# A new order for the first third of an RWKV block with a squared-ReLU feed-forward, and a last product in two column runs

## The chip, the cores and the metric

The kernel runs on one core of one Trainium2 chip. The metric is the device time of one execution, in microseconds (us); lower is better. TensorE (PE) multiplies matrices, VectorE (DVE) and ScalarE (ACT) read its results out of PSUM, GpSimd (POOL) works on SBUF alone and issues some DMAs, SyncE (SP) issues most of them.

## What is computed

```python
# attention part: B, H, S, D = 4, 8, 768, 48
for t in range(S):
    kt, vt, rt = k[:, :, t], v[:, :, t], r[:, :, t]
    cur = np.einsum('bhd,bhe->bhde', u[None] * kt, vt)
    y[:, :, t] = np.einsum('bhd,bhde->bhe', rt, state + cur)
    state = w[None, :, :, None] * state + np.einsum('bhd,bhe->bhde', kt, vt)

# feed-forward part on x = y as [3072 tokens, 384]: w_in [384, 2048], w_out [2048, 384]
h = np.maximum(x @ w_in, 0.0)
out = h * h @ w_out
```

Inputs and the output are float32; the matrix products run in bf16 with float32 sums.

## The kernel before

**Units.** The sequence is cut into 6 chunks of 128 steps; with 4 batches that makes 24 units of 128 tokens and all 8 heads. Unit i is batch i % 4, chunk i // 4, so units 0 to 3 start from a zero state and unit i needs the state that unit i - 4 left. The recurrence is done per unit as small matrix products. The steps of one unit i are:

- `ld.r.i`, `ld.k.i`, `ld.v.i`: loads of 192 KB each (pieces of 192 bytes), on SyncE's queue
- `rh.i`, `kh.i`: r and k times the decay tables, into bf16; `P0.i`, `P1.i`, `du.i`, `dv.i`: the term of the step's own token (r*k, times u, summed, times v); `vb.i`: v in bf16
- `T.i` (eight transposes on TensorE) and `Tc.i` (their copy out of PSUM), or `XB.i` (a transposing DMA) in their place for later units; `A.i` (eight products), `Bm.i.0`, `Bm.i.1` (their mask), `Y.i` (the unit's output), `U.i` (its share of the state), `S0`/`ts`/`S` (the state's update)
- `xs.i` adds the own-token term; `X.i` and `xTc.i`, or the DMA `xX.i`, bring the result into the layout that the feed-forward part needs

**Feed-forward part.** Units are grouped (`GROUPS`: two groups of one unit, then eleven of two). `F1.g.s` computes 512 columns of `x @ w_in` into one PSUM bank: 12 products of 128 columns for a group of one, 6 products of 256 columns for a group of two. `re.g.s` is the ReLU out of PSUM, `sq.g.s` the square. `F2.i.q` is a quarter of unit i's second product: four matmuls of 384 columns; four quarters sum into one bank, `os.i` copies it out and `out.i` stores it.

**Weights.** `w_in` is eight pieces W1[0..7]. `lW.0.s` loads a piece as float32 on SyncE's queue (384 KB, four buffers `wsa`) and `cW.0.s` casts it; piece 2 comes by `W.0.2`, a casting DMA that GpSimd issues. `w_out` is four pieces by `W.1.0` to `W.1.3`, all casting DMAs of GpSimd. F1 of a one-unit group's piece s needs W1[2s] and W1[2s+1], F1 of a two-unit group's piece s needs W1[s]; `F2.i.q` needs W.1.q.

**What sets the order.** `ORDER` is one written-out list of all steps. A token reads `what:engine/buffers`: `A.1:P/1/2` is step A of unit 1 on TensorE into PSUM buffers 1 and 2; the engine letters are A (ScalarE), D (VectorE), G (GpSimd), P (TensorE) and S (SyncE's DMA queue); a D or A with a digit picks a form of `sq`. Each engine runs its steps in the list's order and waits at a step until the data and the buffer that it names are ready. PSUM has four general buffers (`bank`), two for F1 (`bankH`) and two for F2 (`bankO`). `Z.n.b` are n dummy products into a bank, which only keep TensorE working in the first microseconds.

The last unit to finish is 22. Its four quarters run last on TensorE. Its eviction is cut in two halves of 192 columns, `os.22.0` on ScalarE and `os.22.1` on VectorE, both out of the same PSUM bank, with a store behind each.

## Time and profile before

| | |
|---|---|
| three runs | 175.53, 175.57, 176.38 us; median 175.57 |
| the profiled execution: span from first to last instruction | 174.6 us; the runs' median is 0.9 us longer than this span |
| granted TensorE clock, mean | 0.998 |
| busy: PE, DVE, ACT, POOL | 164.3, 140.6, 109.4, 69.4 us |
| DMA traffic | 28.36 MB, mean 162 GB/s |
| SyncE's queue | 72.6% of the 16 DMA engines' span |
| GpSimd's queue | 6.3% |
| first F1 product starts | 21.63 us into the span |
| last product ends | 171.09 us into the span |

The profile's times are microseconds from the first instruction. PE is the row of matrix products, PEld that of the weight loads into the array, which overlap them. The 40 slices are equal parts of the span, with busy shares in tenths. A line of a timeline has the start, the length, the engine and the line of the kernel, and in brackets the idle time before it and what ended it. A DMA's landing is when its last engine reports.

### The profile page before, as it was taken

What the parts mean: (1) busy time and instruction counts of PE and PEld (TensorE: products, weight loads), DVE (VectorE), ACT (ScalarE), POOL (GpSimd) and SP (SyncE); (2) the same over time, 40 slices, a digit from 0 to 9 for tenths busy, and PEclk for the clock granted to TensorE, in tenths of its full rate; (3) what the DMA queues carried; (4) which work ended last, traced back from release to release, by engine and by line L of the source; (5) the groups of instructions that cost most, each with busy time, mean ns of one, the idle gap of its engine ahead of it and who ended that gap; (6) DMA issues with size and microseconds to landing.
All of it is one profiled execution on the core that took longest, in us unless ns stands there. A gap on an engine that the chain in (4) does not pass through costs nothing.

```text
span 174.6 us, 4605 instructions
## 1 busy us (share of the span) xinstructions
PE 164.3 (94%) x1813; PEld 127.1 (73%) x1813; DVE 140.6 (80%) x279; ACT 109.4 (63%) x203; POOL 69.4 (40%) x85
## 2 busy tenths in 40 slices
PE   3978599999999999999999999999999999999991
PEld 3967488866778777877767787777778677787760
DVE  5779677799899989999989898899988667853620
ACT  3578479549499987786677669669478142164410
POOL 5253834044366594925373960700950302000000
PEclk9999999999999999999999999999999999999999
DMA  4989999989799999999998989989931422110041
GB/s 99 228 194 240 320 200 237 207 155 213 144 205 177 231 217 165 233 157 252 152 214 187 195 164 220 160 196 230 164 94 26 158 90 71 24 45 4 0 165 61
DMA packets 102421, 28.36 MB, mean 162 GB/s; under 512 B 94840, under 2 KB 102400, under 8 KB 102400
## 3 DMA queue, kind: packets, MB, share of 16 engines
q1 hardware_dynamic: 100504, 26.20, 72.6%
q0 software_dynamic: 1744, 1.77, 6.3%
q8 instruction: 14, 0.23, 0.5%
q10 hardware_dynamic: 152, 0.10, 0.2%
q14 instruction: 7, 0.06, 0.1%
HBM read 20.46 MB, written 4.72 MB: 144 GB/s over the span
## 4 chain that ended last, share of the span: by engine, by line
PE 84%; DMA 6%; SPq 4%; POOL 1%; issue 1%; ACT 0%; DVE 0%; POOLq 0%
PE bank L472 36%; PE bank L445 36%; DMA wsa<-in_moe_w_in_dram 6%; SPq L320 4%; PE bank L376 3%; PE bank L394 2%; PE bank L392 2%; PE bank L403 2%; PE bank L363 2%; PE bank L429 1%; POOL W L262 1%; SPq L324 0%; POOL urow L218 0%; ACT vb L260 0%; DVE os L262 0%
## 5 line engine op out<-in xcount | busy, mean ns | idle before, releaser
L445 PE MATMUL bank<-xT,W 128*128 128x256 bf16 (+1 forms) x624 | 74.4, 264 | 2.3 <-ACT W L260 2.1
L472 PE MATMUL bank<-W,hq 128*128 128x384 bf16 x384 | 73.6, 326 | 0.0
L453 ACT ACTIVATE hr<-bank 128x512 bf16<-128x512 f32 x71 | 42.0, 597 | 36.8 <-PE bank L445 34.2
L445 PEld LDWEIGHTS <-W 128*128 128x128 bf16 x624 | 55.4, 98 | 12.6 <-ACT W L260 2.2
L472 PEld LDWEIGHTS <-hq 128*128 128x128 bf16 x384 | 35.6, 98 | 17.8
L460 ACT ACTIVATE hq<-hr 128x512 bf16<-128x512 bf16 x57 | 34.7, 629 | 2.5 <-DVE hr L455 2.2
L384 DVE TENSOR_TENSOR Bm<-bank,maskJT 128x512 bf16<-128x512 f32 x48 | 31.4, 682 | 3.1 <-PE bank L376 3.0
L346 POOL TENSOR_TENSOR P<-P,ub 128x384 f32<-128x384 f32 x14 | 15.2, 1087 | 30.2 <-DVE P L342 27.4
L354 POOL TENSOR_TENSOR dv<-ldv,du 128x384 f32<-128x384 f32 x19 | 16.4, 874 | 25.0 <-DVE du L349 21.0
L455 DVE TENSOR_SCALAR hr<-bank 128x512 bf16<-128x512 f32 x25 | 17.1, 688 | 11.2 <-PE bank L445 7.5
L464 DVE TENSOR_TENSOR hq<-hr 128x512 bf16<-128x512 bf16 x35 | 15.0, 456 | 1.7 <-ACT hr L453 1.7
L411 DVE TENSOR_TENSOR xs<-bank,dv 128x384 bf16<-128x384 f32 x24 | 13.2, 553 | 3.2 <-PE bank L394 2.5
L481 PE MATMUL bank<-identity 128*128 128x128 bf16 x139 | 11.1, 244 | 2.7 <-POOL identity masks.py:199 2.7
L260 ACT COPY os<-bank 128x384 f32<-128x384 f32 (+1 forms) x18 | 8.4, 469 | 8.1 <-PE bank L472 8.1
L342 POOL TENSOR_TENSOR P<-ldr,ldk 128x384 f32<-128x384 f32 x11 | 11.3, 1025 | 4.8 <-DMA ldr<-in_r_dram 4.8
L349 DVE TENSOR_REDUCE du<-P 128x8 f32<-128x384 f32 x24 | 12.9, 542 | 0.0
L260 ACT COPY rkT<-bank 128x1024 bf16<-128x1024 bf16 x10 | 10.1, 1016 | 3.4 <-PE bank L363 3.3
L481 PEld LDWEIGHTS <-identity 128*128 128x128 bf16 x139 | 9.8, 112 | 2.9 <-POOL identity masks.py:199 2.7
L424 POOL TENSOR_TENSOR S0W<-ts,WLm 128x384 bf16<-128x384 f32 x7 | 7.4, 1061 | 10.0 <-PE bank L472 6.7
L394 PE MATMUL bank<-vb,Bm 128*128 128x48 bf16 x192 | 10.8, 183 | 0.5 <-ACT vb L260 0.5
L394 PEld LDWEIGHTS <-Bm 128*128 128x128 bf16 x192 | 9.5, 96 | 1.5 <-issue 0.8
L260 ACT COPY xT<-bank 128x384 bf16<-128x384 bf16 x14 | 6.5, 478 | 5.1 <-PE bank L429 5.1
(62 smaller groups left out, 167.1 us busy)
## 6 DMA issues: line engine op xcount, KB each, us to landing
ldr<-in_r_dram SPq DMA_DIRECT2D x24, 192.0 KB, 3.8
ldk<-in_k_dram SPq DMA_DIRECT2D x24, 192.0 KB, 3.9
ldv<-in_v_dram SPq DMA_DIRECT2D x24, 192.0 KB, 3.6
out_dram<-os SPq DMA_DIRECT2D x23, 192.0 KB, 2.1
wsa<-in_moe_w_in_dram SPq DMA_DIRECT2D x7, 384.0 KB, 5.9
W<-in_moe_w_out_dram POOLq DMA_DIRECT2D x4, 384.0 KB, 7.6
rkT<-rk SPq DMA_TRANSPOSE x14, 4.2
W<-in_moe_w_in_dram POOLq DMA_DIRECT2D x1, 192.0 KB, 8.8
```

The costliest lines, as they stand in the source:

```text
L260: e.copy(o, a)
L346: e.tensor_mul(t, t, ub)
L354: e.tensor_mul(dvb[slot[f"dv{i}"]], loaded("v", i), t)
L384: e.tensor_mul(Bmb[slot[f"Bm{i}{h}"]], heads(bank(f"bA{i}{h}"), 128), mask_b)
L394: e.matmul(y[:, hc, D * h : D * (h + 1)], m[h][:, hc, :], vb[:, 2 * hc + h, :], start=(c == 0), stop=True, skip_group_check=True,)
L445: e.matmul(hp[:, fi, :], W1[f // 2][:, c, 128 * (f % 2) : 128 * (f % 2 + 1)], xt[:, c, :], start=(c == 0), stop=(c == CCH - 1), skip_group ...
L453: e.activation(hr, hp, AF.Relu)
L455: e.tensor_scalar_max(hr, hp, 0.0)
L460: e.activation(hq, hr, AF.Square)
L464: e.tensor_mul(hq, hr, hr)
L472: e.matmul(bank(f"bO{i}", "bO")[:, 0:d_model], hqb[slot[f"hq{g},{f // m}"]][:, at : at + L], W2[q][:, f % 4, :], start=(f == 0), stop=(f = ...
L481: e.matmul(banks[b][:, 0:128], identity, identity, start=True, stop=True, skip_group_check=True)
```

## The change

1. The list `ORDER` is new from its beginning to about `F1.5.1` (a third of all steps). Behind that each engine has the same steps in the same order, with other buffer numbers. The count of dummy products is the same, 139; six of them now stand behind F1.1.0. Some 70 steps of the first third move to another engine: GpSimd has 89 steps where it had 72, ScalarE 189 where it had 204. All loads are on SyncE's queue, as they were, in a new order.
2. `F2.22.0` to `F2.22.3` are replaced by `F2c.22.0` and `F2c.22.1`: the whole sum of 16 matmuls for columns 0 to 255, then for columns 256 to 383, in two PSUM banks. Each is copied out and stored by itself, and `os.23` and `out.23` stand between.

The beginning of the list before, to the last product of units 0 and 1:

```
ld.r.1:S/0 w:A ld.k.1:S/0 u:S Z.48.5:P tab:A ld.k.0:S/1 ld.k.2:S/2 shw:D ld.r.0:S/1 logw:A ld.r.2:S/2 Wt:A/0 P0.1:D/0
shu:D Wk:A/1 lW.0.6:S/0 rh.1:D/0 kh.1:D ld.v.1:S/0 ld.k.3:S/3 T.1:P/0 kh.0:D/1 Z.16.5:P P1.1:G Tc.1:A/0 kh.2:D/2 rh.0:D
ld.v.3:S/1 WtS:A rh.2:D P0.2:G/1 A.1:P/1/2 WkS:A T.0:P/3 lW.0.1:S/1 Z.16.5:P P1.2:D ld.r.3:S/3 Tc.0:A/1 du.1:D/0
P0.0:D/2 cW.0.6:A ld.v.0:S/2 A.0:P/0/3 dv.1:G Bm.1.1:D/0 Z.6.5:P du.2:D/1 T.2:P/2 P1.0:G Bm.1.0:D/1 ld.v.2:S/3 Z.22.5:P
Tc.2:A/2 Bm.0.0:D/2 Bm.0.1:D/3 lW.0.0:S/2 vb.1:A/0 lW.0.5:S/3 kh.3:D/3 Y.1:P/1 cW.0.1:A lW.0.7:S/0 A.2:P/0/2 xs.1:D/0
Z.4.5:P P0.3:G/3 vb.3:A/1 du.0:D/2 lW.0.4:S/1 X.1:P/3 Z.8.5:P rh.3:D wc:S xTc.1:A/0 Bm.2.0:D/4 vb.0:A/2 T.3:P/1
ld.k.4:S/4 dv.0:D Y.0:P/3 Z.13.5:P Tc.3:A/3 vb.2:G/3 Bm.2.1:D/5 P1.3:G xs.0:D/1 A.3:P/0/2 X.0:P/1 cW.0.0:A U.0:P/3
dv.2:G Bm.3.0:D/1 Z.6.7:P xTc.0:A/1 du.3:D/3 lW.0.3:S/2 F1.1.0:P/0 Bm.3.1:D/0 ld.r.4:S/4 F1.0.0:P/1 re.1.0:D/0 W.1.0:G
W.0.2:G cW.0.7:G Y.2:P/0 Y.3:P/1 re.0.0:A/1 ld.k.5:S/5 xs.2:D/2 cW.0.5:A dv.3:D F1.1.3:P/0 cW.0.4:A X.2:P/2 F1.0.3:P/1
re.1.3:D/2 ld.r.5:S/5 xTc.2:A/0 W.1.1:G U.2:P/0 xs.3:D/3 F1.0.2:P/0 re.0.3:A/3 sq.1.3:D2/0 WLcol:A X.3:P/2 F1.1.2:P/1
re.0.2:D/4 xTc.3:A WLm:G U.3:P/1 F1.2.1:P/0 re.1.2:A/5 W.1.2:G sq.0.3:A0/1 F1.2.5:P/1 re.2.1:D/2 W.1.3:G sq.0.0:A0/2
U.1:P/2 S0.2:D re.2.5:A/3 F1.2.4:P/0 sq.0.2:D2/3 cW.0.3:A S0.0:D F1.2.7:P/1 re.2.4:D/1 sq.1.0:A0/4 F2.0.0:P/1
sq.2.5:D2/5 re.2.7:A/4 S0.3:D F1.0.1:P/0 F1.2.3:P/1 re.0.1:D/0 F2.1.0:P/0 S0.1:D re.2.3:A/3 F1.1.1:P/0 sq.1.2:D2/6
sq.0.1:D2/7 ld.k.7:S/6 F1.2.0:P/1 re.1.1:A/5 F2.0.1:P re.2.0:A/0 sq.1.1:D2/8 F1.2.2:P/0 sq.2.4:A0/9 sq.2.0:D1/10
F2.1.1:P kh.4:D/4 F1.2.6:P/1 ld.v.5:S/4 rh.4:D P0.4:D/4 F2.1.2:P ld.r.7:S/6 re.2.2:D/5 P1.4:G F2.0.2:P re.2.6:D/1
sq.2.2:A0/11 F2.1.3:P ld.v.4:S/5 kh.5:G/5 sq.2.1:A0/12 sq.2.6:D1/13 F2.0.3:P os.1:A/0 du.4:D/4 ld.k.6:S/0 T.4:P/0
...
```

and the same stretch after:

```
w:A tab:A ld.r.2:S/0 ld.k.3:S/0 shw:D ld.r.1:S/1 logw:A Wk:A/0 Z.48.4:P Z.22.5:P ld.r.0:S/2 Wt:A/1 u:S rh.1:D/0
ld.k.1:S/1 shu:D kh.1:D rh.2:D/1 WtS:A T.1:P/0 ld.k.2:S/2 ld.k.0:S/3 Z.13.4:P rh.0:D/2 Tc.1:A/0 P0.1:G/0 ld.r.3:S/3
kh.3:D/3 lW.0.1:S/0 A.1:P/1/2 Z.16.5:P Z.4.4:P P1.1:G kh.0:D T.0:P/3 P0.2:G/1 wc:S lW.0.0:S/1 ld.v.1:S/0 Bm.1.1:D/0
ld.v.0:S/1 P0.0:G/2 lW.0.6:S/2 P0.3:G/3 kh.2:D P1.3:G Tc.0:A/1 Z.16.5:P Bm.1.0:D/1 rh.3:D du.1:D/0 T.2:P/0 ld.v.2:S/2
vb.1:A/0 Tc.2:A/2 A.0:P/2/3 Z.8.4:P lW.0.5:S/3 Bm.0.1:D/2 T.3:P/1 dv.1:G cW.0.0:A WLcol:A Z.6.5:P P1.2:D P1.0:G
Bm.0.0:D/3 vb.0:G/1 Y.1:P/0 du.0:D/1 A.2:P/3/2 xs.1:D/0 du.2:D/2 dv.0:G WLm:G Bm.2.1:D/4 ld.v.3:S/3 X.1:P/0 Y.0:P/2
Bm.2.0:D/5 xs.0:D/1 du.3:D/3 cW.0.1:A U.0:P/3 xTc.1:A/0 Tc.3:A/3 vb.2:G/2 lW.0.7:S/1 A.3:P/2/0 X.0:P/1 S0.0:D F1.1.0:P/0
Bm.3.0:D/1 cW.0.6:G vb.3:A/3 dv.2:G xTc.0:A/1 cW.0.5:G Y.2:P/3 lW.0.4:S/0 WkS:A U.3:P/2 Bm.3.1:D/0 re.1.0:A/0 cW.0.7:A
U.1:P/1 F1.0.0:P/1 xs.2:D/2 ld.r.4:S/4 dv.3:G ld.k.4:S/4 Y.3:P/0 W.0.2:G cW.0.4:G kh.4:G/4 S0.3:D Z.6.4:P lW.0.3:S/2
re.0.0:A/1 X.2:P/3 W.1.0:G F1.1.3:P/0 xs.3:D/3 ld.k.5:S/5 F1.0.3:P/1 sq.1.0:D2/0 W.1.1:G rh.4:D sq.0.0:D2/1 W.1.2:G
X.3:P/2 xTc.2:A/0 cW.0.3:G re.1.3:A/2 F1.0.2:P/0 ld.r.5:S/5 ld.v.4:S/4 re.0.3:A/3 xTc.3:A sq.0.3:D2/2 re.0.2:A/4
F1.1.2:P/1 W.1.3:G ld.v.5:S/5 T.4:P/0 F1.2.1:P/0 kh.5:G/5 P0.5:G/4 re.1.2:D/5 sq.1.3:D2/3 P0.4:G/0 Tc.4:A/4 re.2.1:D/0
F1.2.5:P/1 A.4:P/3/2 sq.2.1:D2/4 re.2.5:A/1 F1.2.7:P/0 F1.2.4:P/1 re.2.7:A/3 U.2:P/0 re.2.4:A/2 F1.0.1:P/0 F1.1.1:P/1
ld.k.6:S/6 sq.1.2:D2/5 sq.0.2:D2/6 ld.r.6:S/6 Bm.4.1:D/3 rh.5:D Bm.4.0:D/2 P1.4:G re.0.1:A/0 S0.2:D T.5:P/2 vb.5:G/4
sq.0.1:D2/7 F1.2.2:P/0 re.1.1:A/5 F1.2.3:P/1 Tc.5:A/5 A.5:P/3/0 F2.1.0:P/0 ld.r.7:S/1 ld.k.7:S/1 re.2.2:A/4 S0.1:D
ld.v.6:S/6 sq.1.1:A0/8 P1.5:D Bm.5.1:D/5 vb.4:A/5 re.2.3:A/0 F1.2.6:P/0 F2.0.0:P/1 F2.1.1:P Bm.5.0:D/4 U.4:P/2 du.4:D/4
Y.4:P/1 dv.4:D xs.4:D/4 sq.2.2:A0/9 F1.2.0:P/1 F2.0.1:P re.2.0:D/5 X.4:P/0 du.5:D/0 F2.0.2:P F2.1.2:P ld.k.9:S/3 Y.5:P/3
sq.2.0:D1/10 U.5:P/1 re.2.6:D/4 dv.5:G F2.0.3:P F2.1.3:P xs.5:D/0 ts.5:D/0 rh.6:D/6 ld.v.7:S/0 sq.2.3:D2/11 kh.6:G
...
```

The last steps and the code:

```diff
-F2.20.3:P sq.12.5:A0/0 F2.23.1:P os.20:D/2 F2.23.2:P out.20:S F2.23.3:P out.19:S F2.22.0:P/1 out.21:S os.23:D/1
-F2.22.1:P out.23:S F2.22.2:P F2.22.3:P os.22.0:A/2 os.22.1:D out.22.0:A out.22.1:S
+F2.20.3:P sq.12.5:A0/2 F2.23.1:P os.20:D/2 F2.23.2:P out.20:S F2.23.3:P out.19:S out.21:S F2c.22.0:P/1 os.23:D/3
+out.23:S os.22.0:A/2 out.22.0:A F2c.22.1:P/0 os.22.1:D out.22.1:S
...
+        def F2c(e, i, h):
+            g, j = group_of[i]
+            n = len(GROUP[g])
+            m = 4 // n
+            c = part(h)
+            for f in range(FCH):
+                at = L * n * (f % m) + L * j
+                e.matmul(
+                    bank(f"bO{i}{h}", "bO")[:, c],
+                    hqb[slot[f"hq{g},{f // m}"]][:, at : at + L],
+                    W2[f // 4][:, f % 4, c],
+                    start=(f == 0), stop=(f == FCH - 1), skip_group_check=True,
+                )
...
         def os(e, i, half=None):
             c = part(half)
-            copy(e, osb[slot[f"os{i}"]][:, c], bank(f"bO{i}", "bO")[:, c])
+            o = f"bO{i}" if half is None else f"bO{i}{half}"
+            copy(e, osb[slot[f"os{i}"]][:, c], bank(o, "bO")[:, c])
...
     def part(half):
-        return slice(0, d_model) if half is None else slice(d_model // 2 * half, d_model // 2 * (half + 1))
+        return slice(0, d_model) if half is None else (slice(0, 256), slice(256, d_model))[half]
```

## The prediction

> **What bounds the kernel now.** I read the page first, then the trace stage by stage, then its two ends. Of the page, the engines' shares, two rows of the 40 slices, and the start of the chain of work that ended last:

> ```profile
> PE 164.3 (94%) x1813; PEld 127.1 (73%) x1813; DVE 140.6 (80%) x279; ACT 109.4 (63%) x203; POOL 69.4 (40%) x85
> ...
> PE   3978599999999999999999999999999999999991
> ...
> DMA  4989999989799999999998989989931422110041
> ...
> PE 84%; DMA 6%; SPq 4%; POOL 1%; issue 1%; ACT 0%; DVE 0%; POOLq 0%
> ```

> TensorE (PE) is the bound from the sixth slice on; before that the chain runs through loads. The table by stage says where it turns (length, PE busy, then weight loads, VectorE, ScalarE, POOL; granted clock, DMA share, GB/s):

> ```profile
> 16.00:21.60 5.60, 3.25 (x59) 2.60 (x56) 4.41 (x9) 2.99 (x6) 4.84 (x6) 1.00 0.99 293
> 21.60:24.20 2.60, 2.30 (x47) 2.13 (x48) 1.45 (x3) 1.37 (x3) 0.97 (x2) 1.00 1.19 198
> 24.20:45.00 20.80, 20.80 (x239) 16.23 (x240) 17.91 (x35) 14.69 (x28) 8.04 (x11) 1.00 1.08 202
> 45.00:75.00 30.00, 30.00 (x357) 23.84 (x353) 28.46 (x53) 25.82 (x49) 19.61 (x21) 1.00 1.06 198
> ```

> From 24.2 on PE has no hole, and the DMA engines are full (1.08) until about 75. So the order can win only in front of 24.2, and lose anywhere behind. The timeline shows the first feed-forward product F1.1.0 (x24, with F1.0.0) and what released it:

> ```profile
> 20.70 0.86 ACT L260 CAST W<-wsa 128x768 bf16<-128x768 f32 x1 [2.61 <-DMA wsa<-in_moe_w_in_dram]
> ...
> 21.63 1.51 PE L445 MATMUL bank<-xT,W 128*128 128x128 bf16 x24 [2.06 <-ACT W L260]
> ...
> 24.15 0.51 PE L445 MATMUL bank<-xT,W 128*128 128x128 bf16 x6 [0.27 <-POOL W L262]
> ```

> W1[0] was the last thing needed. I measure by a *packed start*: when PE would have begun had everything from F1.1.0 on run without a hole. At 24.15 it had done F1.1.0, F1.0.0 (0.67 each), Y.2, Y.3 (0.2 each) and half of F1.1.3 (0.34), together 2.08, so the packed start is 22.07. To the last product's end at 171.09 that leaves 149.0 us of packed work, which the change keeps, but for one Z.6 (six dummy products, 6 x 0.056 = 0.33 us) that now stands behind F1.1.0.

> The end, from the timeline:

> ```profile
> 171.09 0.32 ACT L260 COPY os<-bank 128x192 f32<-128x192 f32 x1 [4.72 <-PE bank L472]
> ...
> 171.44 0.36 DVE L262 COPY os<-bank 128x192 f32<-128x192 f32 x1 [2.39 <-ACT os L260]
> 171.83 0.33 SPq L489 DMA_DIRECT2D out_dram<-os  x1
> ```

> The two halves of the last eviction read one bank and run one after the other; the last store lands 1.65 after its issue, at 173.48, and the span ends at 174.64. The median is 175.57, so 0.93 us lies outside the span; I sum against 174.64 and carry the difference over.

> **The tail.** Instead of 16 products of 384 columns at 0.163 (2.60), F2c runs 16 of 256 at the grouped F1's pitch of 0.109 (1.74) and 16 of 128 at the single F1's 0.0555 (0.89): +0.03. The first run's copy and store lie under the second. After the last product stands one copy of 128 columns; from 556 ns at 384 and 356 at 192 (1.04 ns a column) it takes 0.29, where 0.32 + 0.03 + 0.36 stood: -0.42. F2c.22.1 waits for os.23 (0.56), hidden under F2c.22.0's 1.74. Tail: **-0.39**. [...]

> **The front.** Loads were on SyncE's queue before as well; only their order is new. Eight r/k loads now stand ahead of all v, and W1[1] and W1[0] right behind them. A 192 KB load takes the full DMA 0.8 to 1.0 us, a 384 KB weight load 1.2 to 1.3 (spacing of landings). So W1[0], 20.68 before, lands near 14: that wait is gone. But v.1, which landed at 11.63, has two more loads, one more weight load and wc ahead of it: +2 x 0.9 + 1.25 + 0.3, so about 14.9 (13.4 if its slowest DMA engine doesn't lag by the 1.4 that it did).

> What comes late next is ScalarE's queue behind v.1. Back to back, by its rows: vb.1 0.42, Tc.2 0.92, cW.0.0 0.8, WLcol 0.5, cW.0.1 0.8, xTc.1 0.4, Tc.3 0.92: about 20.1. On PE, A.3 and X.0 wait for Tc.3 and stand ahead of F1.1.0, which starts near 20.7 instead of 21.63. Then the banks: Y.2, U.3 and Y.3 wait for VectorE's S0.0, Bm.3.0, Bm.3.1 (to 22.4); Z.6 lies in such a hole and costs nothing; F1.1.3 waits for cW.0.7 (ScalarE, 23.0) and X.2 (23.6). Packed start by then 23.6 - 2.25 = 21.35.

> POOL has 89 steps for 72. Behind dv.1 at 14.9 its rows add up to: dv.1 0.83, P1.0 1.0, vb.0 0.58, dv.0 0.83, WLm 0.74, vb.2 0.58, cW.0.6 0.87, dv.2 0.83, cW.0.5 0.87, dv.3 0.83, so W.0.2 (before at 20.54) is issued near 22.7, cW.0.4 ends at 24.4. Then kh.4 (1.0) waits for k.4. The twelve loads and six weight loads ahead of it were through most DMA engines at 22.4 before, and have the same work now; r.4 and k.4 add 0.9 each, the slowest engine about 1.1: near 25.3; **behind it on POOL stand W.1.0, W.1.1, W.1.2, cW.0.3 and W.1.3**, the whole second weight matrix, issued from 26.3 where it was from 19.65. POOL's own DMAs take the engines when they run; from 22.3 to 36.3 the traffic by queue was

> ```profile
> q0 software_dynamic: 1742, 1.77, 77.7%
> q1 hardware_dynamic: 4094, 1.11, 38.3%
> ```

> A W.1 transfer took 7.3 from issue to landing, the following ones landed 2.3 to 2.5 apart. So: 33.6, 36.05, 38.5, 40.8. Their users F2.1.0, F2.1.1, F2.0.2, F2.0.3 stand 12.3, 14.3, 17.0 and 18.85 us of packed work behind F1.1.0 (T 0.45, A 0.44 with its switch, Y.4 0.4, F1 0.66, F2 0.65): packed starts 21.3, 21.75, 21.5, **21.95**. W1[2] (W.0.2) at F1.0.1, 8.8 in: landing 30.0 by 7.3, 31.5 by the 8.8 that it took behind another, so 21.2 to 22.7; I take 21.2, as it is now first in its queue. The latest decides: 21.95, that is **-0.12** against 22.07; bounds 20.9 (v.1 and k.4 without lag) to 23.4 (k.4 as late as its 26.81 of before).

> Behind that, engines change hands in units 6 to 11 (kh, P0, vb to POOL, os.4/os.5 to VectorE) at equal work; PE covers them as it did before, taken at zero; if a cover is gone, one POOL product is 1.0.

> Sum: -0.12 - 0.39 = **-0.5: 174.1 span, 175.1**.

> **Rivals.**
> 1. *Faster, 173.9.* v.1 at 13.4 and k.4 at 23.7 take the front to 20.9: -1.2 - 0.4. For it: the landings of loads ahead of the first weight load lagged under 0.9. Against it: the lag grew at the first weight load.
> 2. *Slower, 176.6.* kh.4 holds the weights up: k.4 at 26.8 puts W.1.3 at 42.3 and the packed start at 23.4: +1.4 - 0.4. It decides if W.1.3 lands after 42.2. For it: k.4 took 8.4 before. Against it: POOL's transfers, which slowed it then, start later now.
> 3. *Slower, 178.5.* T.5, which stood behind F2.0.3 and now stands ahead of F2.1.0, waits for unit 5's loads. It is due 10.1 packed, at 32; k.5 and r.5 took 13 us beside POOL's transfers. Issued at 22 they would land at 34.7; +0.8 for kh.5 or rh.5, 25.4 packed. Against it: POOL's traffic starts at 28, after they should be through.
> 4. *Slower, 176.5.* PE is over half idle from 15 to 20.7, since the Zs now stand earlier; if its clock drops to half, some 2 us of products take double: +1.9 less the gain. The page of before shows full clock through its 2.06 hole. [...]

> **Chances.** Forecast 0.35, rival 1 0.26, rival 2 0.22, rival 3 0.10, rival 4 0.07. About 0.5% (0.9 us) is what this kernel's measurement can tell from none. Faster by more: rival 1 and 0.06 of the forecast, 0.32. Within: the rest of the forecast and 0.05 of rivals 2 and 4, 0.34. Slower: 0.34. The forecast's own range is 174.3 to 176.0; with rivals 1, 2, 4 and half of 3, 173.6 to 177.6.

> **What would show it.** F1.1.0 near 20.7, released by X.0 or Tc.3, not by a weight cast; W.1.0 issued near 26 and landing near 33.5; no PE wait over 0.5 behind 45; one DVE copy of 128 columns behind the last product. Wrong if PE waits on kh.5/rh.5 at T.5, on a v load, or shows a granted clock under 1.0 near 20.

## The result: 182.29 us, 3.6% slower, and the profile after

The kernel after takes 182.29 us (median of five runs, 181.78 to 184.12) beside 176.38 us of the kernel before on the same chip (175.53 to 177.42): a ratio of 1.036 [1.030, 1.041]. The prediction was 175.1, with a range up to 177.6. A ratio here leaves out the runs of a kernel that lie over 1.5% above its fastest and a median counts them all, so for a kernel whose runs scatter the two differ. The profiled execution is the slowest of the five, 184.12 us with a span of 182.4 (before: 176.38 with 174.6). The page:

```profile
PE 167.1 (92%) x1829; PEld 130.1 (71%) x1829; DVE 146.5 (80%) x277; ACT 102.4 (56%) x188; POOL 86.9 (48%) x102
...
PE   4895798599989899799999999999999999999993
...
PEclk9999569999999999999999999999999999999999
DMA  5999999989897998989859899978982414301032
...
PE 74%; DVE 13%; DMA 4%; SPq 3%; ACT 2%; issue 2%; POOL 1%; DVEq 0%; ACTq 0%; POOLq 0%
```

Three things are new: the granted clock (PEclk) falls to about half in the fifth and sixth slices, PE's row has fives to eights up to the seventeenth slice where it had nines from the sixth on, and VectorE (DVE) holds 13% of the chain. The table by stage (length, busy of PE, weight loads, VectorE, ScalarE, POOL; granted clock, DMA share, GB/s):

```profile
16.00:21.60 5.60, 3.12 (x45) 2.33 (x45) 4.41 (x10) 4.45 (x9) 5.26 (x10) 0.78 1.01 272
21.60:24.20 2.60, 2.60 (x34) 2.60 (x32) 1.91 (x4) 2.31 (x4) 2.60 (x4) 0.50 0.93 213
26.00:33.90 7.90, 5.20 (x84) 4.79 (x82) 6.44 (x9) 4.16 (x7) 7.80 (x10) 1.00 1.21 190
45.00:75.00 30.00, 27.19 (x300) 20.15 (x296) 29.28 (x46) 17.04 (x31) 25.91 (x25) 1.00 0.93 184
```

Three stages lose. From 21.6 to 24.2 PE is full, at half clock. From 26 to 33.9 it has 5.20 of 7.90. From 45 to 75, where before it had 30.00 of 30.00, it has 27.19, with VectorE at 29.28 and ScalarE down from 25.82 to 17.04.

The second of these, from 26 to 33.9, in the timeline (start, length, engine, line, operation; in brackets the idle time before it):

```profile
29.27 0.72 POOL L333 DMA_DIRECT2D W<-in_moe_w_out_dram  x1
...
29.71 3.49 DVE L464 TENSOR_TENSOR hq<-hr 128x512 bf16<-128x512 bf16 x1
30.01 1.01 POOL L336 TENSOR_TENSOR rk<-ldk,Wkhat 128x384 bf16<-128x384 f32 x1
...
30.96 1.94 POOL L342 TENSOR_TENSOR P<-ldr,ldk 128x384 f32<-128x384 f32 x2
...
33.12 0.68 DVE L455 TENSOR_SCALAR hr<-bank 128x512 bf16<-128x512 f32 x1
...
33.85 0.38 PE L445 MATMUL bank<-xT,W 128*128 128x256 bf16 x2 [2.70 <-DVE hr L455]
```

The square sq.1.3, whose shortest form takes 0.41 us, takes 3.49. It stands beside kh.5, P0.5 and P0.4, which follow each other on POOL without a gap, and ends 0.29 us behind the last of them. When it began, POOL was still issuing the transfer W.1.3 (29.27 to 29.99). The ReLU re.2.1 (33.12) had to wait behind it, and PE waited 2.70 us for the bank that re.2.1 empties.

The end:

```profile
178.46 0.37 ACT L260 COPY os<-bank 128x256 f32<-128x256 f32 x1 [3.87 <-PE bank L486]
...
179.35 0.29 DVE L262 COPY os<-bank 128x128 f32<-128x128 f32 x1 [2.08 <-PE bank L486]
179.67 0.33 SPq L504 DMA_DIRECT2D out_dram<-os  x1
```

Last product to end of span: 3.09 us, where it was 3.55.

**The sum of the two traces.** By the prediction's packed starts: F1.1.3 stands at 26.04, so 23.8 against 22.07 (+1.7, of which 0.33 is Z.6, which the prediction had laid into a hole); F1.2.7 at 33.85, so 26.5 (+2.7 more), and it is still 26.5 at F2.0.3 (45.34). From F2.0.3's start to the end of the last product there are 133.97 us, for 130.15 of packed work (149.0 - 18.85): +3.8. The tail gives 0.46 back. Together +7.8, which is the difference of the spans. The typical run after is 1.8 us shorter than the profiled one. If its last part is the same, its F2.0.3 stands near 43.5 (an estimate), so its front loses 2.6 and not 4.4.

### The profile page after: what moved, and what is told of

It reads as the page before. It is cut to its first block, busy times and chain, and to the rows that moved or that the text cites. A ratio compares the mean times of both kernels' runs of the same rounds, so it can differ in the third digit from the quotient of the medians.

```text
span 182.4 us, 4643 instructions
## 1 busy us (share of the span) xinstructions
PE 167.1 (92%) x1829; PEld 130.1 (71%) x1829; DVE 146.5 (80%) x277; ACT 102.4 (56%) x188; POOL 86.9 (48%) x102
## 3 DMA queue, kind: packets, MB, share of 16 engines
q0 software_dynamic: 1744, 1.77, 5.8%
HBM read 20.46 MB, written 4.72 MB: 138 GB/s over the span
## 4 chain that ended last, share of the span: by engine, by line
PE 74%; DVE 13%; DMA 4%; SPq 3%; ACT 2%; issue 2%; POOL 1%; DVEq 0%; ACTq 0%; POOLq 0%
PE bank L445 32%; PE bank L472 29%; DVE hq L464 4%; PE bank L376 3%; DMA ldv<-in_v_dram 3%; PE bank L394 2%; SPq L320 2%; PE bank L403 2%; PE bank L392 2%; DMA ldk<-in_k_dram 2%; PE bank L486 1%; DVE dv L354 1%; DVE xs L411 1%; DVE rk L339 1%; DVE Bm L384 1%
## 5 line engine op out<-in xcount | busy, mean ns | idle before, releaser
L445 PE MATMUL bank<-xT,W 128*128 128x256 bf16 (+1 forms) x624 | 76.0, 268 | 4.1 <-DVE hr L455 2.7
L453 ACT ACTIVATE hr<-bank 128x512 bf16<-128x512 f32 x75 | 44.3, 598 | 48.3 <-PE bank L445 43.3
L472 PE MATMUL bank<-W,hq 128*128 128x384 bf16 x368 | 70.5, 326 | 0.5 <-DVE hq L464 0.5
L445 PEld LDWEIGHTS <-W 128*128 128x128 bf16 x624 | 56.5, 100 | 14.6 <-issue 4.5
L472 PEld LDWEIGHTS <-hq 128*128 128x128 bf16 x368 | 34.3, 98 | 17.4 <-DVE hq L464 0.6
L460 ACT ACTIVATE hq<-hr 128x512 bf16<-128x512 bf16 x49 | 29.9, 629 | 0.0
L354 POOL TENSOR_TENSOR dv<-ldv,du 128x384 f32<-128x384 f32 x17 | 15.4, 912 | 27.0 <-DVE du L349 25.9
L464 DVE TENSOR_TENSOR hq<-hr 128x512 bf16<-128x512 bf16 x43 | 23.7, 575 | 2.0 <-ACT hr L453 2.0
L455 DVE TENSOR_SCALAR hr<-bank 128x512 bf16<-128x512 f32 x21 | 14.4, 689 | 8.7 <-PE bank L445 5.2
L342 POOL TENSOR_TENSOR P<-ldr,ldk 128x384 f32<-128x384 f32 x17 | 17.8, 1055 | 5.7 <-DMA ldk<-in_k_dram 5.7
L260 ACT COPY os<-bank 128x384 f32<-128x384 f32 (+1 forms) x16 | 7.6, 473 | 13.6 <-PE bank L472 9.7
L260 ACT COPY rkT<-bank 128x1024 bf16<-128x1024 bf16 x10 | 10.1, 1010 | 6.6 <-PE bank L363 6.6
L336 POOL TENSOR_TENSOR rk<-ldk,Wkhat 128x384 bf16<-128x384 f32 x11 | 12.1, 1101 | 1.0 <-PE bank L403 0.6
```

The source lines that it names most:

```text
L260: e.copy(o, a)
L342: e.tensor_mul(P0b[slot[f"P{i}"]], loaded("r", i), loaded("k", i))
L354: e.tensor_mul(dvb[slot[f"dv{i}"]], loaded("v", i), t)
L445: e.matmul(hp[:, fi, :], W1[f // 2][:, c, 128 * (f % 2) : 128 * (f % 2 + 1)], xt[:, c, :], start=(c == 0), stop=(c == CCH - 1), skip_group ...
L453: e.activation(hr, hp, AF.Relu)
L460: e.activation(hq, hr, AF.Square)
```

## The experiments

All are edits of the list; times are medians, and ratios are against the kernel before, timed beside the edit on the same chip. First a table of what the traces and the runs gave, with two columns that part the front from the rest (the start of F2.0.3, and from there to the end of the last product). Waits of PE are given as the profile has them; the recorded expectations count each about 0.16 us longer, from when the next product could have started.

| kernel | F1.1.3 | F2.0.3 | from there to PE's end | median us | ratio |
|---|---|---|---|---|---|
| after | 26.04 | 45.34 | 133.97 | 182.29 | 1.036 [1.030, 1.041] |
| x2_warm | 23.75 | 44.81 | 133.97 | 183.61 | 1.046 [1.039, 1.053] |
| x3_swap | 26.22 | 44.28 | 133.88 | 183.11 | 1.041 [1.035, 1.047] |
| x11_first | 26.77 | 47.35 | 133.68 | 184.45 | 1.040 [1.033, 1.047] |
| x14_run | 25.40 | 43.02 | 134.61 | 181.69 | 1.031 [1.025, 1.037] |
| x6_squares | 25.86 | 44.25 | 130.60 | 180.00 | 1.023 [1.015, 1.032] |
| x9_all | 23.93 | 42.53 | 130.26 | 178.41 | 1.013 [1.006, 1.021] |
| x10_mended | 24.85 | 43.61 | 130.25 | 179.94 | 1.013 [1.006, 1.020] |
| x13_mended2 | 23.49 | 45.68 | 130.25 | 178.01 | 1.012 [1.007, 1.018] |
| x15_v4 | 23.84 | 41.03 | 130.80 | 180.19 | 1.008 [1.003, 1.013] |

**x1_tail: the order of before with the new end.**

```diff
-F2.22.0:P/1 ... os.23:D/1 F2.22.1:P out.23:S F2.22.2:P F2.22.3:P os.22.0:A/2 os.22.1:D out.22.0:A out.22.1:S
+F2c.22.0:P/1 os.23:D/1 out.23:S os.22.0:A/2 out.22.0:A F2c.22.1:P/0 os.22.1:D out.22.1:S
```

> The order of before up to the last unit, with the changed kernel's two column runs at the end. Prediction's sum for the tail: 0.4 us shorter than the kernel before (ratio 0.998), one copy of 128 columns of 0.29 us behind the last product. [...]

175.90 us beside 176.13, ratio 1.001 [0.997, 1.005]. In its trace the span ends 3.18 us behind the last product, 0.4 earlier than before, as the sum had it. The time can't show it: in that trace PE also stood 0.66 us at F1.0.2 for the cast cW.0.4, which waited 0.73 us for its load; in the profile of before it followed the cast ahead of it without a wait.

**x2_warm: hold the clock.**

```diff
+Z.18.5:P (ahead of Y.1)  +Z.11.5:P (ahead of X.1)  +Z.9.5:P (ahead of Y.0)  +Z.5.5:P (ahead of A.3)
```

> The changed kernel with 43 dummy products more, put where TensorE waited: 18 before Y.1, 11 before X.1, 9 before Y.0, 5 before A.3. Theory 1 (TensorE was too idle from 15.5 to 19.1 and so ran at half clock from 19.1 to 25.9): the granted clock stays at 1.0, F1.1.3 starts near 23.7 instead of 26.0, and T.4 is then held by kh.4 at 26.2, so 2.3 us less there; what is left of it at the end depends on the wait behind sq.1.3, which may move to T.5: 1.0 to 2.4 us less than the changed kernel, ratio to before 1.022 to 1.030. Rival (the front is held by loads and by ScalarE's queue, the clock only fell beside them): F1.1.3 still near 25.5 and no gain.

The clock stays full there and F1.1.3 comes 2.3 us earlier, but the time is no better: 183.61 us, a ratio of 1.046 where 1.022 to 1.030 was expected. At F2.0.3 only 0.5 of the 2.3 is left: another square, sq.0.2, now stands beside the same three POOL products and takes 3.31 us, T.5 waits 1.49 us for Bm.4.1 and 0.29 us for rh.5, both behind it in VectorE's queue, and the clock halves at 35.26 instead. One run of the kernel after itself had a granted clock of 1.00 and still took 181.78. So the half clock is real, but in this order what it costs is owed again at the next wait.

**x8_cold: take the dummy products out of the kernel before.**

```diff
-Z.4.5:P -Z.8.5:P -Z.13.5:P -Z.6.7:P
```

> The kernel before without four of its filler runs on TensorE, Z.4.5, Z.8.5, Z.13.5 and Z.6.7 (31 small products between 15 and 21 us whose results nothing uses). Theory (TensorE that is busy for less than about a third of some 3.4 us gets half its clock for the next 3.4 or 6.8 us, though no single pause is that long): the granted clock falls to 0.5 for 3.4 or 6.8 us, beginning between 17 and 22 us, the first products F1.1.0 to F1.1.3 run at a pitch of about 107 ns, and the time rises by 1.5 to 2.5 us over that of the kernel before. Rival (the drop in the kernel after has a cause outside of these runs): clock 1.0 throughout, same time as before within 0.5 us, or a little less.

177.30 us beside 175.77, ratio 1.008 [1.003, 1.012]: 1.5 us, as expected. The clock is half for 6.83 us from 18.77, F1.1.0 runs at 107 ns a product. In the traces of before and after the pitch of the dummy products falls from 107 to 56 ns at 6.60 and 5.45 us, where the record of the clock first has it full; windows of 3.41 us are counted from there. The kernel before, then x8_cold, then after:

```profile
16.84:20.25 3.41, 2.41 (x45) 1.84 (x42) 3.39 (x7) 1.26 (x2) 2.96 (x5) 1.00 0.94 294
20.25:23.66 3.41, 2.03 (x45) 2.04 (x46) 1.09 (x3) 1.73 (x3) 1.48 (x3) 1.00 1.16 257
```

```profile
15.36:18.77 3.41, 1.91 (x34) 1.27 (x31) 3.41 (x8) 2.94 (x5) 1.61 (x3) 1.00 0.88 216
18.77:22.18 3.41, 2.04 (x22) 1.59 (x21) 2.20 (x4) 1.25 (x2) 3.22 (x4) 0.50 1.04 313
```

```profile
15.70:19.11 3.41, 1.03 (x19) 0.64 (x18) 2.29 (x5) 3.34 (x8) 3.13 (x6) 1.00 1.02 269
19.11:22.52 3.41, 3.01 (x35) 2.60 (x36) 3.34 (x7) 2.33 (x4) 3.35 (x6) 0.50 1.00 279
```

In the fourteen traces other than x7_late's the changes of clock up to 56 us lie on this grid, which starts with the clock's first rise, at 5.45 to 8.70 us. The full clock halved eleven times, each time behind a window with PE busy 0.57 to 1.98 us; it stayed full behind two windows with 1.80 and 1.87 and behind all with 2.03 or more. So in these traces busy time gives no sharp limit: both outcomes lie between 1.80 and 1.98, and the third of a window (about 1.1 us) that the expectation took is too low. No single pause had to be long: in the kernel after the longest in that window is 1.2 us. The kernel before passes with 2.03, which is next to nothing above it, and it does not always pass: of its 70 executions that were timed beside the edits, eight have a granted clock of 0.988 to 0.990, as one halved window would give, and take 176.66 to 178.32 us.

**x3_swap, x11_first, x14_run: the row of products on POOL.** Three edits in the kernel after:

```diff
 x3_swap:   -W.1.3:G ... kh.5:G/5 P0.5:G/4          +kh.5:G/5 W.1.3:G P0.5:G/4
 x11_first: -re.1.2:D/5 sq.1.3:D2/3 ... re.2.1:D/0  +re.1.2:D/5 re.2.1:D/0 sq.1.3:D2/3
 x14_run:   -P0.5:G/4 -P0.4:G/0                     +Bm.4.0:D/2 P0.4:D/0 P0.5:D/4
```

> The changed kernel with one step moved: GpSimd issues W.1.3 behind kh.5 instead of in front of it, so that its three products kh.5, P0.5, P0.4 no longer run back to back. Theory 2 (VectorE's sq.1.3, with two inputs in SBUF, waits as long as GpSimd's products follow each other without a break): sq.1.3 ends near 30.7 instead of 33.2, F1.2.7 starts near 31.3 instead of 33.9, up to 2.5 us less at the end, ratio 1.021 to 1.028. Rival (the weights' transfers or their issue slow VectorE): sq.1.3 still takes 3 us or more, as the transfers of W.1.0 to W.1.2 run on and W.1.3 only comes later; no gain.

> The kernel after with two neighbours on VectorE exchanged: re.2.1, which empties a bank (its operand lies in PSUM), goes ahead of sq.1.3, which multiplies two operands in SBUF. Theory (only a VectorE step with two SBUF operands is held up by a run of products on GpSimd, and the hole of 2.7 us at F1.2.7 came from re.2.1 standing behind such a step): re.2.1 takes its 0.7 us beside GpSimd's run, F1.2.7 starts at about 31.3 us (33.85 in the kernel after), sq.1.3 is held up as before, up to 0.3 us behind the end of a product of GpSimd; the steps that are then late (sq.2.1, rh.5, T.5) give part of it back, so F2.0.3 comes 1 to 2 us earlier than 45.3 and the time is 180.5 to 181.5. Rival (every VectorE step is held up while GpSimd works, or the hole has another cause): re.2.1 takes over 2 us too, F1.2.7 at 33 us or later, time 182.3.

> The kernel after with one thing changed: P0.5 and P0.4 run on VectorE, behind Bm.4.0, instead of on GpSimd directly behind kh.5. Theory (the row of three products on GpSimd is what held sq.1.3 for 3.5 us): sq.1.3 ends about 0.3 us behind kh.5 and takes at most 1.6 us, F1.2.7 starts 5.5 to 6.2 us behind F1.1.3 (7.8 in the kernel after), F2.0.3 17.2 to 18 us behind F1.1.3 (19.3 in the kernel after), and the time falls by 1.3 to 2.2 us to 180 to 181. Rival (sq.1.3 is held by something else): sq.1.3 takes over 2 us, same time as after.

In x3_swap POOL issues a transfer (W.1.3) behind kh.5, so that 0.7 us without a product lie between kh.5 and P0.5:

```profile
29.19 1.21 POOL L336 TENSOR_TENSOR rk<-ldk,Wkhat 128x384 bf16<-128x384 f32 x1
...
30.07 0.61 DVE L464 TENSOR_TENSOR hq<-hr 128x512 bf16<-128x512 bf16 x1
30.35 0.76 POOL L333 DMA_DIRECT2D W<-in_moe_w_out_dram  x1
30.85 0.69 DVE L455 TENSOR_SCALAR hr<-bank 128x512 bf16<-128x512 f32 x1 [0.17 <-ACT rkT L260]
```

sq.1.3 is through 0.28 us behind kh.5's end, and F1.2.7 starts at 31.60. The next squares then meet P0.5 and P0.4 (0.86, 1.21 and 1.21 us), and of the 2.25 us 1.06 are left at F2.0.3. The time shows no gain: 183.11 us, a ratio of 1.041 where 1.021 to 1.028 was expected. In x11_first re.2.1 takes 0.69 and F1.2.7 starts 5.0 us behind F1.1.3 (7.8 after), but the squares behind it are held in turn (2.33, 1.21, 1.22), rh.5 comes at 37.06, and the clock halves a second time: 184.45, a miss. In x14_run, without the row, F1.2.7 starts 5.4 and F2.0.3 17.6 us behind F1.1.3 (19.3 after), about as expected, but not for the reason expected: kh.5 ran from 31.03 on, a microsecond later than in the kernel after, so sq.1.3 (29.06 to 29.48) stood beside no POOL product and took its 0.41. The test of sq.1.3 beside kh.5 alone did not take place there, and the early gain is in part luck. The ratio falls by half a point, less than the width of its interval, and the time not by the 1.3 to 2.2 us.

What is held, and until when, is the same in the fourteen traces other than x7_late's. In these, 61 squares on VectorE between 24 and 75 us take 0.3 us or more over their 0.41. Of these 55 end 0.27 to 0.30 us behind the end of a POOL step that works on SBUF; the other six, of 1.04 to 1.09 us, stand beside POOL's issue of the transfers of W.1. In all 61 cases POOL was already at a step or an issue when the square began. The mask products Bm on VectorE, which read PSUM, are not held: the 461 in these traces that overlap a POOL step take 0.67 to 0.69 us, as the 211 others do. In x9_all the mask products Bm (1.27 for two) and S0.2 (0.54, where before has 0.55) run beside P0.5 and P0.4 at their usual length, while the square beside P1.4 takes 1.22:

```profile
31.01 2.00 POOL L342 TENSOR_TENSOR P<-ldr,ldk 128x384 f32<-128x384 f32 x2
...
31.11 1.27 DVE L384 TENSOR_TENSOR Bm<-bank,maskJT 128x512 bf16<-128x512 f32 x2
...
32.31 0.54 DVE L418 TENSOR_TENSOR S0W<-bank,WLm 128x384 bf16<-128x384 f32 x1
...
33.09 0.99 POOL L346 TENSOR_TENSOR P<-P,ub 128x384 f32<-128x384 f32 x1
33.14 1.22 DVE L464 TENSOR_TENSOR hq<-hr 128x512 bf16<-128x512 bf16 x1 [0.29 <-ACT hr L453]
```

The runs agree on who is held; by what in the hardware, no run here shows. A row of three GpSimd products held one square through all three in the kernel after (3.49 us) and in x2_warm (3.31), but not always: in x6_squares and x11_first the square came through behind the second (2.10 and 2.33 us).

**x6_squares, x7_late, x5_engines: the stage from 45 to 75 us.** x6 moves seven squares to ScalarE, x7 and x5 give the steps the engines of before, x7 from F2.2.0 on (39 steps), x5 from T.4 on (53):

```diff
 x6_squares: -sq.2.3:D2 -sq.2.4:D2 -sq.2.5:D2 -sq.3.1:D2 -sq.3.0:D2 -sq.3.5:D2 -sq.4.1:D2
             +sq.2.3:A0 +sq.2.4:A0 +sq.2.5:A0 +sq.3.1:A0 +sq.3.0:A0 +sq.3.5:A0 +sq.4.1:A0
```

> The kernel after with seven squares of units 2 to 4 (sq.2.3, sq.2.4, sq.2.5, sq.3.1, sq.3.0, sq.3.5, sq.4.1) moved from VectorE to ScalarE at their places. Theory (between 45 and 75 us the products of VectorE and those of GpSimd get in each other's way, and VectorE, 29.3 us busy of 30, is what TensorE waits for): TensorE's holes between 48 and 74 us fall from 4.1 us to about 2, VectorE's stretch from 8.3 us to 4 or less, and the time falls by about 2 us against the kernel after, to some 180.3; the two losses before 48 us stay. Rival (late loads of units 6 to 11 make the holes, whatever engine squares): the holes stay at about 4 us and the time at 182.3.

> The kernel after, in which each step from F2.2.0 on (45 us) runs on the engine that it had in the kernel before; 39 steps change engine, the order stays. Theory (the products are dealt out badly between VectorE and GpSimd in this stage): holes between 48 and 74 us fall from 4.1 us to 1.5 to 2, time down by 2 to 2.5 us to about 180. Rival (the order or the late loads make the holes): holes and time stay (182.3 us).

> The changed kernel's order, but from T.4 on every step on the engine (and in the form of square) that it had before: 53 steps change hands, GpSimd's load goes back. Theory 3 (from 45 to 75 us VectorE is full, and steps of VectorE and GpSimd stretch each other: 8.3 us of stretch on VectorE where before had 3.0): the holes of 4.1 us on TensorE between 48 and 74 fall to 1 or less, sq.1.3 still waits (kh.5 stays on GpSimd, P0.5 and P0.4 leave it, so its wait falls to 1 us or so): 3 to 5 us less than the changed kernel, ratio 1.008 to 1.018. Rival (the holes come from the order or from late loads, not from who does the steps): they stay, ratio above 1.025.

x6_squares takes 180.00 us, 2.3 less than after, as expected; the intervals of the two ratios still touch, between 1.030 and 1.032, but the traces are clear. PE has its stage back, with ScalarE taking the work that VectorE gave up:

```profile
45.00:75.00 30.00, 29.69 (x320) 22.54 (x319) 27.05 (x47) 23.50 (x44) 24.76 (x24) 1.00 0.97 193
```

From F2.0.3 on it needs 130.60 us where after needs 133.97, and each kernel with these squares on ScalarE has 130.25 to 130.80. With the squares on VectorE it stayed 133.9 to 134.0 when F2.0.3 came 0.5 or 1.1 us earlier (x2, x3), and x6_squares has the same loads in the same order, so late loads don't make the loss. VectorE's groups in this stage say which steps grew. After:

```profile
L464 DVE TENSOR_TENSOR hq<-hr 128x512 bf16<-128x512 bf16 x7 | 5.7, 815 | 0.0
L384 DVE TENSOR_TENSOR Bm<-bank,maskJT 128x512 bf16<-128x512 f32 x8 | 5.2, 678 | 0.0
...
L339 DVE TENSOR_TENSOR rk<-ldr,Wt 128x384 bf16<-128x384 f32 x3 | 2.8, 928 | 0.0
```

and before:

```profile
L384 DVE TENSOR_TENSOR Bm<-bank,maskJT 128x512 bf16<-128x512 f32 x10 | 6.5, 681 | 0.3 <-PE bank L376 0.3
...
L339 DVE TENSOR_TENSOR rk<-ldr,Wt 128x384 bf16<-128x384 f32 x5 | 3.0, 613 | 0.0
...
L464 DVE TENSOR_TENSOR hq<-hr 128x512 bf16<-128x512 bf16 x3 | 1.8, 610 | 0.0
```

The masks, out of PSUM, keep 0.68 us; the squares and rh grow. Summed over the stage, VectorE's steps take about 8 us more than their shortest forms, against about 3 before, with eight steps fewer; in x6_squares 4.7 (4 or less was expected). x7_late took 180.3 to 182.7 us in three runs, so its gain, if there is one, is a third of what was expected; in its profiled execution (a span of 217.3 us) the clock was granted at 0.75 from 8 us on, but for one window at half, so its trace tells nothing of the holes. x5_engines is a miss, 183.0 to 188.4: with vb.5 on ScalarE as before, that engine waited 6.2 us for v.5 (landed at 39.83) in front of re.1.1, and the clock halved again. The stage behind improved in part: in the 30 us from F2.0.3 on, VectorE's steps take 4.3 us over their shortest forms where the kernel after has 8.2, and from F2.0.3 to PE's end it needs 132.55 us.

**x9_all, x10_mended, x13_mended2, x15_v4: all of it together.** x9 has x2's and x6's edits, x3's swap, rh.5 behind re.2.1, and four early squares on ScalarE; x10 reorders the early squares; x13 also puts P0.5 and P0.4 on VectorE; x15 moves one load:

```diff
 x9_all:      +sq.1.3:A0/3 +sq.2.1:A0/4 +sq.1.2:A0/5 +sq.0.2:A0/6   re.2.1:D/0 rh.5:D
 x10_mended:  re.0.2:A/4 sq.0.2:A0/6 ... re.1.2:D/5 sq.0.0:D2/1 ... Tc.4:A/4 sq.1.2:A0/5 re.2.1:D/0 sq.0.3:D2/2 rh.5:D
 x13_mended2: rh.4:D sq.1.0:D2/0 ... Bm.4.0:D/2 P0.4:D/0 P0.5:D/4
 x15_v4:      ld.v.4:S/4 lW.0.3:S/2 ... ld.r.5:S/5   (x13: lW.0.3:S/2 ... ld.r.5:S/5 ld.v.4:S/4)
```

> The kernel after with all three suspected losses taken out: four filler runs (Z.18.5, Z.11.5, Z.9.5, Z.5.5) put before Y.1, X.1, Y.0 and A.3 to hold the clock; early on GpSimd kh.5, then the issue of W.1.3, then P0.5 and P0.4, rh.5 moved up behind re.2.1 on VectorE, and the squares sq.1.3, sq.2.1, sq.1.2, sq.0.2 on ScalarE; and the seven later squares on ScalarE. Theory (clock 1.7 us, the run of products on GpSimd 2.7 us, engines after 45 us 4 us; the end gains 0.4): F1.2.7 starts at about 29.4 us, T.5 at about 32, F2.0.3 at about 42 (45.3 in the kernel after), holes between 48 and 74 us about 2 us, time 176 to 177, level with the kernel before. Rival (behind these losses the loads of W.1 and of units 4 and 5 would hold TensorE anyway): F2.0.3 not before 44, time about 180.

> The kernel of the run x9_all with the three holes that its trace still shows between 27.8 and 36 us (0.82, 0.50 and 0.77 us) attacked: on VectorE re.1.2 and re.2.1 go ahead of the squares sq.0.0 and sq.0.3 and rh.5 follows them, on ScalarE sq.0.2 goes ahead of Tc.4 and sq.1.2 directly behind it. Theory (each of these holes is an emptying of a bank that stands behind a square in its engine's queue): F2.0.3 starts at 40.5 to 41 us (42.5 in x9_all), no hole over 0.5 us is left, and the time falls by 1.5 to 2 us to 176.4 to 177, level with the kernel before (ratio 0.998 to 1.008). Rival (the transfers of W.1.1, landing at 34.8 us, and of units 6 and 7 hold TensorE next): F2.0.3 after 42 us, time 178.

> The kernel of the run x10_mended with GpSimd's run of products broken up instead of moved among: P0.5 and P0.4 go to VectorE (behind Bm.4.0), so that of kh.5, P0.5 and P0.4 only kh.5 is left on GpSimd; rh.4 goes ahead of sq.1.0. Theory (a VectorE step with two SBUF operands ends 0.3 to 0.45 us behind the end of the GpSimd product beside it, or of the last of a row of products): sq.0.3 is held to about 0.3 us behind kh.5's end and nothing on VectorE behind it, rh.5 ends within 1 us of kh.5, T.5 starts without a hole over 0.6 us, F2.0.3 at 41 to 41.8 us if vb.1 starts at 15.2 us (20.3 to 21 us behind F1.0.0's start; in x10_mended 20.1, in x9_all 20.0 with F1.0.0 less late), PE ends 1.5 us earlier than in x9_all (172.8 us), and the time is 176.5 to 177.5. Rival (VectorE is now the bound, with two products more): T.5 after a hole of over 1 us, time 178 to 180 as before.

> The kernel of the run x13_mended2 with one load moved on SyncE's queue: ld.v.4 goes ahead of lW.0.3 (it was behind ld.r.5, was issued at 25.0 to 28.3 us there, and landed at 39.6 us behind the three transfers of W.1; in x9_all, issued at 24.6 to 25.9, it landed at 30.3). Theory (what is left of the loss once clock, GpSimd and squares are mended is this race between loads of the early units and W.1): v.4 lands before 30 us in the trace, U.4 follows F2.1.1 without a hole (3.0 us in x13_mended2), the time falls by 1 to 2 us to 176 to 177 and its spread (177.3 to 180.7 in x13_mended2) narrows. Rival (another load takes v.4's place, k.5 or r.5, each then 0.5 to 1 us later): T.5 after a hole of 1 us or more, time 177.5 to 179 as before.

x9_all: 178.41, clock full, no hole of note behind 50, F2.0.3 at 42.5 (about 42 expected); the time is 1.4 above the expected range, and PE still waits 1.6 us between 28 and 36 (0.66, 0.33 and 0.61). x10_mended missed, with 179.94 us where 176.4 to 177 was expected (one of its six executions took 345.71 us at full clock, which nothing here explains): its squares went from beside one POOL product to beside another (sq.0.3 1.83, rh.5 2.87 us), and its F2.0.3 is as far behind F1.1.3 as in x9_all (18.8 against 18.6). x13_mended2 removes that, and F2.1.0 starts 11.0 us behind F1.1.3 (12.1 in x9_all, 12.3 in x10_mended). Its time, 178.01, is still above the expected 176.5 to 177.5, and F2.0.3 comes at 45.68 and not at 41 to 41.8, for in the traced execution a load is late:

```profile
PE bank L403 <- ACT vb L260: 2.9, 1, 2.9
```

U.4 waits for v.4, whose issue on SyncE's queue ended at 28.25, after W.1.0's at 27.31; it landed at 39.57, behind W.1.0 to W.1.2. In x9_all the issue ended at 25.91, before W.1.0's, and v.4 landed at 30.32. In x15_v4, issued ahead of lW.0.3, v.4 landed at 25.50. U.4 then follows without a hole, F2.0.3 starts at 41.03 (packed 22.2, where the kernel before has 22.07), and the execution takes 176.61. That is one execution: the twelve lie between 176.61 and 185.85, median 180.19. Five have a granted clock of 0.997 to 1.00 and take 176.6 to 179.0, the others 0.990, 0.981 or 0.972 and 179.8 to 185.9. By the medians x15_v4 is 1.024 times the kernel before (176.03). A window of 3.41 us at half clock takes 0.0096 off the mean over 177 us, so by this estimate these figures mean one to three such windows. The expected narrower spread did not come. Which wait makes those windows is open: the profile is that of a run at full clock. No version is faster than the kernel before: x1_tail equals it, and the interval of every other ratio lies above 1.

## Why the prediction was wrong

**The stations in front were right.** v.1 landed at 15.19 (14.9), Tc.3 ended at 19.98 (20.1, by luck: the rows that the prediction adds up give 19.7, and v.1 was 0.3 late), F1.1.0 started at 21.33 (20.7), cW.0.4 ended at 24.83 (24.4), k.4 landed at 25.03 (25.3), W.1.0 was issued at 26.11 (26.3) and landed at 33.12 (33.6), the next three at 36.88, 39.16, 41.36 (36.05, 38.5, 40.8). Neither kh.4 (rival 2) nor unit 5's loads (rival 3: r.5 landed at 30.0) decided: T.5 started at 36.69 without a wait, since PE had stood earlier, at F1.2.7, for re.2.1 in VectorE's queue.

**The tail was right**, -0.39 against -0.46 in the trace and -0.4 in x1_tail. F2c's second run went at 55.9 ns a product in the trace of after, so the row of F1 (55.5) held.

**Step 1 that failed: "engines change hands at equal work; PE covers them as it did before, taken at zero".** Its own test, no PE wait over 0.5 us behind 45, failed twice (0.58 at U.6, 1.04 at F1.4.7, with 0.41 and 0.47 beside them). It was worth 3.8 us in the trace, and 3.4 of them left with seven squares (x6_squares). Equal work was not equal time here: from 45 to 75 us, with POOL busy 25.91 of the 30, VectorE's squares took 0.82 us in the mean, where their shortest form takes 0.41, and the prediction had the row that hints at it, VectorE already at 28.46 of 30 beside POOL at 19.61, but summed steps and not pairs.

**Step 2: each wait in the packed start was taken for a load or a weight.** Packed starts of 21.3 to 21.95 were worked out from landings; between them the bank's emptying stood behind squares that the sum had at no cost, and Z.6, also at no cost, ran where PE had no hole. "One POOL product is 1.0" as the price of a lost cover was the term mis-sized: sq.1.3 lost 3.1 and F1.2.7 2.7.

**Step 3: rival 4 had the mechanism, at chance 0.07.** PE was busy for 1.03 us of the 3.41 ahead of 19.11, and there the clock halved; with x2_warm's dummy products, and PE busy 3.38 and 2.81 in the windows from 14.77 to 21.60, it stayed full. The price of the half clock was near (+1.9; the packed start moved by 1.7 at F1.1.3, x2_warm won 2.3 there, x8_cold lost 1.5), though 1.9 on the forecast of 175.1 makes 177.0 and not the 176.5 written. What failed was the argument against it, "full clock through its 2.06 hole", which took the length of a hole for the measure; by windows the kernel before had stood at 2.03 of 3.41 us, just above the 1.98 at which the clock halved elsewhere, and in the kernel after no pause in the window ahead of the halving was longer than 1.2 us.

**Shown and argued.** Shown by edits: the loss from 45 us on, and that the squares on VectorE make it (x6_squares); the half clock and its price in the kernel before (x8_cold). Shown by the count over fourteen traces: which steps are held and until when; x3_swap is the one edit that parted the row as planned, and sq.1.3 fell from 3.49 to 0.61 us. Argued: the split of the front's 2.6 to 4.4 us, since its losses don't add up (x2, x3 and x14 each freed 1 to 2.3 us early, and their times show little or none of it), and how much of the late loss is lengthening and how much the bare work of the squares. x15_v4 keeps 6.4 us of lengthening in the 30 us behind F2.0.3 and loses only 0.65 us there, which suggests, but does not show, that here a lengthened step costs time only where VectorE has no slack left.

## What to carry to other kernels

When steps change engines, list which SBUF-only steps of VectorE now run beside which steps of GpSimd, and keep the ones that empty a bank in front of them: here a row of three GpSimd products with no gap cost most (3.49 us for a square of 0.41). Take the share of busy TensorE by windows, here of 3.41 us, and not the longest pause, before calling a clock safe: in the kernel after it halved with no pause over 1.2 us and PE busy 1.03, in the kernel before it stayed full through a hole of 2.06, with PE busy 2.41 and 2.03 in the two windows. Where a front has several nearly equal limits, one mended loss can show up at the next (of x2_warm's 2.3 us 0.5 were left at F2.0.3), so mend them together before judging any.
